# PSUM banks from a table, wider products for the old state, a longer overlap on GpSimd and another order in a chunked linear-attention and gated-MLP kernel

## Chip, core and metric

The kernel runs on one core of a Trainium2 chip. The metric is the device time of one execution in microseconds (us), taken as the median of several runs.

## What is computed

The first half is a linear attention whose state is a 40x40 matrix per head: 4 batches, 8 heads, 768 steps. The second half is an MLP with a spatial gate. Cut to what matters:

```python
for t in range(S):                                     # S = 768, D = 40
    y[:, :, t] = einsum('bhd,bhde->bhe', rt, state)
    Sa = einsum('bhde,bhe->bhd', state, at)
    state = state * wt[:, :, None, :] - einsum('bhd,bhe->bhde', Sa, bt)
    state = state + einsum('bhd,bhe->bhde', vt, kt)
x = y.transpose(0, 2, 1, 3).reshape(B, S, H * D)       # (4, 768, 320)
h = gelu_tanh(x @ w_in); u, v = halves(h)              # 320 -> 1024
v = layernorm(v) * g_ln
v = einsum('ts,bsd->btd', w_sg, v) + b_sg[None, :, None]
out = x + (u * v) @ w_out
```

## The kernel before

The 768 steps are cut into 12 chunks of 64 steps. Within a chunk the recurrence becomes products of matrices with a unit triangular 64x64 matrix per head, which has to be inverted. One unit of work is (c, b): chunk c, batch b, with 8 heads in 4 pairs (NP = 4). Everything in the attention is float32, so each product appears in the trace as two MATMUL records.

The stages of a chunk, with the names that the profile shows:

- The gates, `gate_w` to `gate_t`, work two to three chunks ahead. `gate_1` is a scan of decays on VectorE (`ex`), `gate_2` and `gate_3` scale the inputs (`at`, `kb`, with a second scan into `fixed`), `gate_4` is 32 MATMUL records into two PSUM tiles `ab0` and `ab1`, `gate_t` turns `kb` into the same two tiles. `gate_a` (VectorE), `gate_n` (ScalarE, into `nts`) and `gate_k` (ScalarE, into `kbt`) read those tiles and set them free.
- The inverse of chunk c covers all 4 batches at once. `inv_in` copies two blocks of `nts` on ScalarE, transposes them on VectorE into `n` (STREAM_TRANSPOSE) and sets the start of `x`. `steps` then walks 31 rows: every row is one multiplication into a scratch tile (`tg` for even chunks, `th` for odd ones) and one addition into `x`, both on GpSimd, each needing the one before. The last two rows are done on VectorE, then two transposes, `x1z` and `xt` (`inv_back`). `inv_g` (`gp`), a copy to `gs` on ScalarE (`inv_h`), `inv_x` (`xp`) and copies into `xt` (`inv_y`) finish it.
- `mixed(c, n)` sets GpSimd's order: the last 2*MIX operations of the chunk before (`behind`) are issued in turn with the first 2*MIX of this chunk, one of each, and the rest of this chunk follows alone.
- `chain1` to `chain5` carry the state: `ru` (two groups of products), `vu` on ScalarE, `sp`, `ut`, `pq`, `yp`, with `sc`, `pqs` and `yt` on VectorE and `vs`, `rhsb`, `s`, `vut` on ScalarE. `chain5` writes one PSUM tile `yp`: for every pair p and half h a product with `pqs`, and from chunk 1 on a product of the old state `s` with `rt`, 64 columns each.
- PSUM tiles come from `Banks`: one pool of 6 buffers in rotation during the attention (two more banks hold fixed tiles), 8 later. A tile waits until the tile that had its buffer has been read.

The order of instructions on each engine is fixed in the program. Every step gets a number by hand (tables `CH` and `LAG` for the chains, `GPOS` for the gates, `START` for `inv_in` and `mixed`, `BACK`, `GX` and `GL` for the end of the inverse, `DEC` and `DSTEP` for the splitting of `w_in`, `FILL` and `JUNK` for the first pieces of the MLP), 14 numbers to half a chunk and 28 to a chunk; `half(c, hf, side)` sorts the steps of half a chunk by these numbers and emits them. The numbers are no times: they only set the order. The start has the same in one list (`EX`, `T0` to `TX`, `W16`, `C1`, `SECOND`). `warmup` emits products of a zero tile into a PSUM tile `wp` that nobody reads; `HEADX`, `HEATX` and `HEAT` place them.

While the last inverse runs, `split64` starts to split `w_in` into two float32r parts (`DEC`), partly on GpSimd, through a staging tile `stg` with 3 buffers. All data moves by DMAs that SyncE issues, one queue in order. After chunk 12 `Mlp.run` works off the MLP pieces in the order of `SEQ0` and `SEQ`.

Of the kernel before, what the change touches and what calls it, by code (L numbers as in the profile page):

```python
# [9 lines left out]
F32 = mybir.dt.float32  # L10
# [22 lines left out]
HI_MAX = float(np.uint32(1151 << 20).view(np.float32))  # L33
FIRST = 0
FIRST1 = 0
EW = 1.12
WARM = (14, 0)
T0 = 7.05
T1 = 14.71
T2 = 3.18  # L40
TX = 17.97
LX = 4.92
YM = 64
HEAT = ((11.48, 11),)
# [10 lines left out]
T3 = 12.38
T4 = 17.94
CH = ((-17.8, 4.77, 22.83, 5.29, 40.56, 6.67, 11.98, 12.93, 5.11, 8.75, 12.38, 12.99), (-19.02, -6.94, 39.22, 1.7,
    27.65, 3.73, 7.69, 10.84, -17.0, 8.01, 8.38, 14.21))
GPOS = (((-18.02, -27.66, -4.05, -3.44, 7.45, 13.15, 8.8, 9.52, 9.57, 7.62), (-10.67, -0.89, -0.21, 1.03, 1.09, 8.16,
# [6 lines left out]
GE = ("VVVVV", "VVV", "V", "V")  # L66
START = (12.56, 6.02)
E0A = "GGGG"
E0K = "GVGG"
E1A = "GGGG"  # L70
E1K = "GGGV"
BACK = (20.27, 22.63, 24.69, 25.6)
GX = (25.56, 3.93)
CG = 0.7978845608028654
G1 = 0.044715
ENDS = {(9, 1): (("g", 0.01),), (10, 1): (("r", 0.01),), (11, 0): (("i", 5.0),)}
PIN = 266.02
DSTEP = ((-13.76, -2.78, -0.83, 0.94, 1.02, 4.34), (-10.29, 1.62, 1.75, 2.09, 4.54, 13.69))
DEC = ((264.82, 0), (278.5, 0), (286.65, 0), (289.18, 0), (281.75, 1), (296.38, 1), (293.09, 1), (312.42, 0), (313.95,
    0), (319.1, 1), (328.37, 0), (321.65, 1))  # L80
PX = 266.05
PV = 294.03
PL = 335.9
FILL = (('x0', 0, 321.07), ('v0', 0, 334.89), ('v1', 0, 335.46), ('v2', 0, 345.9), ('u0', 0, 355.78))
# [20 lines left out]
OSTEP = (-3, -1, 0, 0, 0, 0)  # L105
SGE = "GGGGGVGVVVVV"
OUTE = "VVGGGGGG"
SECOND = (32.86, 28.3)
ZERO = (-1, 39.49)
LAST = 2  # L110
MIX = 5
IS = 1
NS = 1
PQ = 1
MK = 40
JUNK = ((307.25, 5), (300.82, 4), (298.83, 6), (300.77, 3), (337.07, 1), (375.48, 3), (391.84, 4))
TP = 1
UT = 0
HEATX = (1000.0, 35.82, 1000.0, 39.48, 1000.0, 85.13, 48.06, 83.96, 1000.0, 1000.0, 1000.0, 166.1, 1000.0, 1000.0,
    1000.0, 1000.0)  # L120
HEADX = (17.16, 15.34, 14.51, 10.1, 1000.0, 24.98, 1000.0, 1000.0, 12.2, 1000.0, 4.58, 1000.0, 13.58, 1000.0, 17.09,
    6.6, 19.94, 1000.0, 19.57, 13.55, 8.17, -1.89, 1000.0, -1.97)
GL = (1.78, 1.2)
LAG = ((15.96, 0.95, -4.98, 0.45, 4.09, 1.29, (1.75, 9.96, -0.51, -0.16), (0.56, 10.54, 1.52, 2.45), 2.4, 1.22, 1.57,
    4.31), (6.29, 2.98, 6.71, 2.27, 9.49, 1.62, (0.64, 4.57, 1.17, 1.89), (5.92, 9.75, 3.57, 6.36), 14.35, 1.68, 5.0,
    8.49))
SEQL = ("s1", "s2", "s0", "s3", "s4", "s5", "s6", "s7", "o0", "o1", "o2", "o3", "o5", "o4")
ROWS = (12, 26)
EX = ((-0.41, 0, 0.35, 0.35, 1.61, 3.07, 2.57, 2.34, 1.25, 1.81), (0.76, 0, 0.75, 0.88, 1.87, 2.83, 3.55, 3.81, 2.13,
    1.97))  # L130


class Banks:

# [43 lines left out]
def attention(tc, a, xd, flag, keep, ps, mlp=None):  # L178
# [3 lines left out]
    V, A, G, T, Q = engines(tc)  # L182
    with ExitStack() as ctx:
# [32 lines left out]
        n = NP * (C + 1)  # L216
# [16 lines left out]
        x0 = iv.tile([128, NQ, 32], F32, name="x0")  # L233
# [72 lines left out]
        gate, unit, x1_of, st2, pqt = {}, {}, {}, {}, {}  # L306
# [1158 lines left out]
```

## Time and profile before

| what | us |
|---|---|
| median of 3 runs | 617.08 |
| runs | 617.08, 617.13, 614.1 |
| the profiled execution | 616.49 |
| span of its profile, first to last instruction | 614.7 |
| TensorE busy (PE) | 569.3 (93%) |
| VectorE busy (DVE) | 490.0 (80%) |
| GpSimd busy (POOL) | 367.3 (60%) |
| ScalarE busy (ACT) | 360.3 (59%) |

The mean granted TensorE clock is 0.956 of the full 2.4 GHz. Four stretches follow each other: a start up to about 73 us, chunks of 24 to 26 us each up to about 300 us, a change-over to the MLP until about 410 us, and the MLP, in which TensorE hardly pauses. The busy time of an engine hides two things that matter here: TensorE's records overlap in a pipeline, so the time from one record's start to the next is its cost and not its duration, and an engine can be short of time in one stretch while its share over the span is low.

### The profile page before, as it was taken

What the parts mean: (1) busy time and instruction counts of PE and PEld (TensorE: products, weight loads), DVE (VectorE), ACT (ScalarE), POOL (GpSimd) and SP (SyncE); (2) the same over time, 40 slices, a digit from 0 to 9 for tenths busy, and PEclk for the clock granted to TensorE, in tenths of its full rate; (3) what the DMA queues carried; (4) which work ended last, traced back from release to release, by engine and by line L of the source; (5) the groups of instructions that cost most, each with busy time, mean ns of one, the idle gap of its engine ahead of it and who ended that gap; (6) DMA issues with size and microseconds to landing.
All of it is one profiled execution on the core that took longest, in us unless ns stands there. A gap on an engine that the chain in (4) does not pass through costs nothing.

```text
span 614.7 us, 24521 instructions
## 1 busy us (share of the span) xinstructions
PE 569.3 (93%) x10136; PEld 519.4 (85%) x10136; DVE 490.0 (80%) x1083; ACT 360.3 (59%) x993; POOL 367.3 (60%) x844
## 2 busy tenths in 40 slices
PE   6888989999999999999976999699999999999995
PEld 5777878889888888887865879698999999999995
DVE  6958989989899899897855987898887679568632
ACT  5446777787787877877735736544453246224410
POOL 6738878888888888888883234455433432333230
PEclk9575999999999999999997999799999999999998
DMA  5613244544444445424415414510121103000002
GB/s 203 171 45 83 85 110 120 148 119 116 128 116 126 115 122 150 119 63 134 118 27 156 109 54 150 164 35 6 34 73 37 34 7 102 2 32 14 20 0 71
DMA packets 56889, 54.06 MB, mean 88 GB/s; under 512 B 35840, under 2 KB 47360, under 8 KB 56768
## 3 DMA queue, kind: packets, MB, share of 16 engines
q1 hardware_dynamic: 56768, 52.40, 30.8%
q8 instruction: 82, 1.34, 1.0%
q14 instruction: 39, 0.32, 0.2%
HBM read 44.52 MB, written 7.86 MB: 85 GB/s over the span
## 4 chain that ended last, share of the span: by engine, by line
PE 55%; DVE 25%; POOL 6%; issue 5%; ACT 4%; DMA 3%; SPq 1%; DVEq 0%; ACTq 0%; POOLq 0%
PE sg L164 13%; PE ru L164 6%; PE ab L164 5%; PE op L164 5%; PE hu L164 5%; PE hv L164 5%; DVE at L164 5%; PE pq L164 4%; PE yp L164 3%; DVE ex L164 3%; DVE fixed L164 3%; POOL x L164 2%; PE sp L164 2%; POOL th L164 2%; PE xp L164 2%
## 5 line engine op out<-in xcount | busy, mean ns | idle before, releaser
L164 POOL TENSOR_TENSOR th<-x,n 128x126 f32<-128x126 f32 (+21 forms) x174 | 66.4, 382 | 21.9 <-DVE n L164 11.7
L164 POOL TENSOR_TENSOR x<-x,th 128x126 f32<-128x126 f32 (+21 forms) x174 | 68.2, 392 | 9.7
L164 PE MATMUL sg<-wsh,vh 128*128 128x384 f32 x192 | 66.1, 344 | 5.6 <-ACT wsh L164 4.5
L164 POOL TENSOR_TENSOR gx<-g,gy 128x384 fp32r<-128x384 f32 x30 | 31.8, 1062 | 64.6 <-ACT gy L164 64.6
L164 PE MATMUL sg<-wsl,vh 128*128 128x384 f32 x192 | 65.8, 343 | 0.5 <-POOL wsl L164 0.5
L164 PE MATMUL sg<-wsh,vl 128*128 128x384 f32 x192 | 65.9, 343 | 0.0
L164 POOL TENSOR_TENSOR x<-x,tg 128x126 f32<-128x126 f32 (+25 forms) x160 | 60.0, 375 | 8.5
L164 POOL TENSOR_TENSOR tg<-x,n 128x126 f32<-128x126 f32 (+25 forms) x160 | 58.1, 363 | 11.3 <-DVE n L164 2.3
L164 PE MATMUL ab<-at,kb 64*64 64x64 f32 x1536 | 40.2, 237 | 13.9 <-DVE kb L164 6.5
L164 PE MATMUL pq<-rt,vut 128*64 128x128 f32 x768 | 52.4, 279 | 0.2 <-ACT vut L164 0.2
L164 DVE TENSOR_TENSOR at<-ab,mask 64x256 f32<-64x256 f32 x96 | 40.4, 421 | 11.8 <-PE ab L164 9.8
L164 PEld LDWEIGHTS ab<-at,kb 64*64 64x64 f32 x1536 | 33.3, 146 | 18.5 <-POOL kbt L164 4.3
L164 PE MATMUL yp<-pqs,kbt 128*64 128x64 f32 x768 | 46.8, 223 | 1.3 <-DVE pqs L164 1.3
L164 ACT CAST gy<-g 128x384 fp32r<-128x384 f32 x30 | 15.4, 514 | 55.4 <-DVE g L164 52.2
L164 ACT CAST vh<-v 128x512 fp32r<-128x512 f32 x24 | 14.9, 621 | 52.7 <-DVE v L164 52.7
L164 PE MATMUL yp<-rt,s 80*64 80x64 f32 (+1 forms) x704 | 43.5, 221 | 1.1 <-issue 1.1
L164 POOL TENSOR_TENSOR vl<-v,vh 128x512 fp32r<-128x512 f32 x24 | 31.4, 1312 | 21.2 <-ACT vh L164 21.2
L164 PEld LDWEIGHTS pq<-rt,vut 128*64 128x64 f32 x768 | 42.2, 139 | 2.1 <-ACT vut L164 0.4
L164 PEld LDWEIGHTS sg<-wsh,vh 128*128 128x128 f32 x192 | 36.9, 192 | 6.5 <-ACT wsh L164 4.8
L164 PEld LDWEIGHTS yp<-pqs,kbt 128*64 128x64 f32 x768 | 39.0, 138 | 2.1 <-DVE pqs L164 2.1
L164 DVE SCALAR_TENSOR_TENSOR g<-sg,gl,bt 128x384 f32<-128x384 f32 x32 | 19.7, 615 | 25.4 <-PE sg L164 24.3
L164 POOL TENSOR_TENSOR rs<-rs,mhalf 128x1 f32<-128x1 f32 x24 | 13.3, 554 | 42.4 <-DVE rs L164 37.1
(169 smaller groups left out, 1746.7 us busy)
## 6 DMA issues: line engine op xcount, KB each, us to landing
main<-main SPq DMA_DIRECT2D x88, 160.8 KB
vs<-vb SPq DMA_DIRECT2D x24, 160.0 KB
vu<-vs SPq DMA_DIRECT2D x24, 160.0 KB
rt<-rt SPq DMA_DIRECT2D x48, 80.0 KB
vut<-vt SPq DMA_DIRECT2D x24, 160.0 KB
xd<-yt SPq DMA_DIRECT2D x96, 40.0 KB
xt<-xd SPq DMA_DIRECT2D x16, 192.0 KB
out<-y SPq DMA_DIRECT2D x16, 192.0 KB
```

Source lines behind the costliest of these rows:

```text
L164: return self.tc.keep_in_program_order(f(*a, **k))
```

## The change

Four things change.

1. `Banks` makes one pool per PSUM bank. A string `BANK` of 503 digits says which bank the n-th tile takes; past its end it goes in rotation. `warmup(0)` takes no tile any more.
2. In `chain5` the old state's share is 4 products of 128 columns per (c, b) (both pairs of a half at once) in place of 8 of 64, and they come behind all products with `pqs`.
3. `MIX` is 7 in place of 5: the last 14 operations of an inverse on GpSimd are issued in turn with the first 14 of the next.
4. Nearly all numbers of the order are new. In the middle chunks, for chunk c in the steady state: TensorE takes `xp` ahead of `gate_4` of the first gate (it came behind `gate_t` of it), `ut` of the chunk's last batch directly behind `gp`, `gate_3` of the first gate on VectorE comes ahead of the next gate's `gate_1`, `n` on VectorE comes ahead of the scan and `kb` of the next gate, and on ScalarE `gate_n` of the last gate stands directly ahead of `inv_in`. At the start, of the 10 pairs of `wp` products that stood behind `chain1` and ahead of the inverse's first products, 6 stand ahead of `chain1` and 2 behind it.

```diff
-EW = 1.12
+EW = 1.14
-T1 = 14.71
+T1 = 22.43
-TX = 17.97
+TX = 22.86
-C1 = 9.42
+C1 = 15.98
-W16 = 3.35
+W16 = 7.12
-START = (12.56, 6.02)
+START = (11.84, 4.21)
-BACK = (20.27, 22.63, 24.69, 25.6)
-GX = (25.56, 3.93)
+BACK = (20.26, 24.86, 29.53, 27.62)
+GX = (26.85, 0.17)
-SECOND = (32.86, 28.3)
-ZERO = (-1, 39.49)
+SECOND = (55.53, 39.82)
+ZERO = (-1, 27.56)
-MIX = 5
+MIX = 7
-GL = (1.78, 1.2)
+GL = (1.02, 3.23)
...
-        self.rings = [ctx.enter_context(tc.tile_pool(name="ps", bufs=6, space=PSUM))] * 6
+        self.pools = [self.bank(i) for i in range(6)]
+
+    def bank(self, i):
+        return self.ctx.enter_context(self.tc.tile_pool(name=f"ps{i}", bufs=1, space=PSUM))
...
     def __call__(self, nm):
+        k = int(BANK[self.n]) if self.n < len(BANK) else self.n % len(self.pools)
         self.n += 1
-        return self.rings[self.n % len(self.rings)].tile([128, 512], F32, tag="ps", name=nm)
+        return self.pools[k].tile([128, 512], F32, tag="ps", name=nm)
...
                         T.matmul(yp[64 * h:64 * h + YM, o], lhsT=kbt[:, l0:l0 + YM], rhs=pqs[:, 4 * (p // 2) + 2 * h + p % 2],
-                                 start=True, stop=True, skip_group_check=True)
-                    for h in range(2 if c else 0):
-                        j = 2 * (p // 2) + h
-                        m = C if j < 3 else D
-                        T.matmul(yp[64 * h:64 * h + m, o], lhsT=st2[b][0:80].rearrange("p j x -> p (j x)")[:, D * j:D * j + m],
-                                 rhs=rt[0:80, p % 2, 2 * (p // 2) + h],
-                                 start=False, stop=True, skip_group_check=True)
+                                 start=not p, stop=True, skip_group_check=True)
+                for j in range(NP if c else 0):
+                    i, h = divmod(j, 2)
+                    m = C if j < 3 else D
+                    T.matmul(yp[64 * h:64 * h + m, 2 * C * i:2 * C * i + 2 * C],
+                             lhsT=st2[b][0:80].rearrange("p j x -> p (j x)")[:, D * j:D * j + m], rhs=rt[0:80, :, j],
+                             start=False, stop=True, skip_group_check=True)
```

`CH`, `LAG`, `GPOS`, `DEC`, `DSTEP`, `FILL`, `JUNK`, `HEADX`, `HEATX` and `EX` change in nearly every number.

## Rows read from the trace of the kernel before

**Rows 1.** Busy time by stretch; us per engine, records, granted clock, DMA.

```profile
147.80:172.45 24.65, 24.08 (x719) 21.39 (x716) 22.57 (x50) 19.68 (x63) 21.51 (x59) 1.00 0.48 124
...
430.00:602.00 172.00, 171.72 (x945) 165.45 (x946) 122.29 (x245) 66.92 (x135) 60.18 (x62) 1.00 0.11 33
```

**Rows 2.** GpSimd in order of time: start, duration, operation, shapes, idle before it.

```profile
142.21 0.24 POOL L164 TENSOR_TENSOR th<-x,n 128x31 f32<-128x31 f32 x1 [0.57 <-DVE n L164]
...
142.94 0.34 POOL L164 TENSOR_TENSOR tg<-x,n 128x78 f32<-128x78 f32 x1
143.24 0.23 POOL L164 TENSOR_TENSOR th<-x,n 128x30 f32<-128x30 f32 x1
...
147.38 0.32 POOL L164 TENSOR_TENSOR th<-x,n 128x78 f32<-128x78 f32 x1
147.78 0.33 POOL L164 TENSOR_TENSOR x<-x,th 128x78 f32<-128x78 f32 x1
...
171.36 0.27 POOL L164 TENSOR_TENSOR x<-x,th 128x45 f32<-128x45 f32 x1
...
172.01 0.32 POOL L164 TENSOR_TENSOR tg<-x,n 128x78 f32<-128x78 f32 x1
```

**Rows 3.** VectorE in order of time, from one x1z to the next.

```profile
147.83 1.09 DVE L164 STREAM_TRANSPOSE x1z<-x 128x512 f32<-128x512 f32 x1
...
163.00 0.69 DVE L164 TENSOR_TENSOR_SCAN fixed<-main,fixed 128x260 f32<-128x260 f32 x1
...
164.68 2.03 DVE L164 STREAM_TRANSPOSE n<-nts 128x1024 f32<-128x1024 f32 x1 [0.27 <-ACT nts L164]
...
172.45 1.10 DVE L164 STREAM_TRANSPOSE x1z<-x 128x512 f32<-128x512 f32 x1
```

**Rows 4.** TensorE in order of time, around one yp.

```profile
148.07 1.07 PE L164 MATMUL pq<-rt,vut 128*64 128x128 f32 x16
148.97 0.28 PE L164 MATMUL yp<-pqs,kbt 128*64 128x64 f32 x4
149.08 0.29 PE L164 MATMUL yp<-rt,s 80*64 80x64 f32 x4
```

**Rows 5.** Groups of the whole span: operation, count, busy us, mean ns, idle before.

```profile
L164 PE MATMUL pq<-rt,vut 128*64 128x128 f32 x768 | 52.4, 279 | 0.2 <-ACT vut L164 0.2
...
L164 PE MATMUL yp<-rt,s 80*64 80x64 f32 (+1 forms) x704 | 43.5, 221 | 1.1 <-issue 1.1
```

**Rows 6.** TensorE, then VectorE, then GpSimd, in the start.

```profile
32.22 7.55 PE L164 MATMUL wp<-warm 128*128 128x128 f32 x40 [0.59 <-ACT kbt L164]
39.70 1.26 PE L164 MATMUL g<-x1z,nts 32*32 32x16 f32 x128
...
34.99 1.07 DVE L164 STREAM_TRANSPOSE x1z<-x 128x512 f32<-128x512 f32 x1
...
43.48 0.24 POOL L164 TENSOR_TENSOR th<-x,n 128x31 f32<-128x31 f32 x1 [9.37 <-DVE n L164]
```

**Rows 7.** GpSimd behind the last inverse, and TensorE's next product.

```profile
321.15 0.72 POOL L164 TENSOR_TENSOR lt<-lt,sc 128x256 f32<-128x256 f32 x1
...
328.47 0.80 PE L164 MATMUL sp<-sc,ident 128*64 128x80 f32 x8 [8.91 <-DVE yt L164]
```

**Rows 8.** TensorE from gp to xp, and ScalarE's copies between them.

```profile
151.07 1.20 PE L164 MATMUL gp<-x1z,nts 32*32 32x32 f32 x64
152.20 0.38 PE L164 MATMUL ru<-ident,sc 104*80 104x104 f32 x2
...
154.05 0.42 PE L164 MATMUL ut<-ident,vu 64*80 64x64 f32 x4
155.04 0.79 PE L164 MATMUL ab<-at,kb 64*64 64x64 f32 x32 [0.57 <-DVE kb L164]
...
156.27 1.20 PE L164 MATMUL xp<-xt,gs 64*32 64x32 f32 x64
...
152.77 1.17 ACT L164 COPY gs<-gp 32x512 f32<-32x512 f32 x2
```

More of the change, by code (lines that the diff above doesn't have):

```diff
@@ L35 @@
 FIRST1 = 0
-EW = 1.12
+EW = 1.14
 WARM = (14, 0)
 T0 = 7.05
-T1 = 14.71
-T2 = 3.18
-TX = 17.97
-LX = 4.92
+T1 = 22.43
+T2 = 3.21
+TX = 22.86
+LX = 4.21
 YM = 64
-HEAT = ((11.48, 11),)
-LV = 5.9
-C1 = 9.42
-WP = 49.4
-W16 = 3.35
+HEAT = ((11.82, 11),)
+LV = 5.13
+C1 = 15.98
+WP = 48.52
+W16 = 7.12
 K16 = 0
-TB0 = -17.46
-TB1 = 16.05
+TB0 = -17.86
+TB1 = 9.57
 CUT0 = (2,)
@@ L54 @@
 ROWS0 = (0, 26)
[L55 to L59, printed above, removed]
[6 rows of a table removed]
+T3 = 8.39
+T4 = 13.75
+CH = ((-14.62, 4.41, 37.47, 6.14, 42.8, 6.77, 12.59, 14.12, 5.17, 9.44, 12.53, 13.26), (-19.81, -6.78, 54.8, 1.73,
+    31.86, 5.06, 7.1, 9.91, -38.88, 7.41, 7.11, 14.02))
+GPOS = (((-22.12, -20.64, -5.86, -5.21, 5.58, 10.09, 7.37, 7.65, 10.04, 6.33), (-18.63, -5.33, -1.99, -1.24, 1.25,
[6 rows of a table added]
 GE = ("VVVVV", "VVV", "V", "V")
-START = (12.56, 6.02)
+START = (11.84, 4.21)
 E0A = "GGGG"
@@ L77 @@
 PIN = 266.02
-DSTEP = ((-13.76, -2.78, -0.83, 0.94, 1.02, 4.34), (-10.29, 1.62, 1.75, 2.09, 4.54, 13.69))
-DEC = ((264.82, 0), (278.5, 0), (286.65, 0), (289.18, 0), (281.75, 1), (296.38, 1), (293.09, 1), (312.42, 0), (313.95,
-    0), (319.1, 1), (328.37, 0), (321.65, 1))
+DSTEP = ((-15.76, -2.54, -1.13, -0.3, 1.65, 2.2), (-13.56, -0.46, 1.98, 3.41, 7.44, 12.01))
+DEC = ((268.49, 0), (278.24, 0), (290.42, 0), (291.86, 0), (282.12, 1), (294.83, 1), (305.79, 1), (316.12, 0),
+    (310.87, 0), (320.78, 1), (326.62, 0), (327.2, 1))
 PX = 266.05
@@ L83 @@
 PL = 335.9
-FILL = (('x0', 0, 321.07), ('v0', 0, 334.89), ('v1', 0, 335.46), ('v2', 0, 345.9), ('u0', 0, 355.78))
+FILL = (('x0', 0, 320.4), ('v0', 0, 333.32), ('v1', 0, 334.58), ('v2', 0, 346.23), ('u0', 0, 360.21))
 AFTER = {"v": (0.56, 0.57, 1.47, 1.57, 2.13, 2.48, 2.96, 4.17, 5.19), "u": (1.14, 1.97, 2.82, 3.17), "x": ()}
@@ L115 @@
 MK = 40
-JUNK = ((307.25, 5), (300.82, 4), (298.83, 6), (300.77, 3), (337.07, 1), (375.48, 3), (391.84, 4))
+JUNK = ((299.01, 5), (309.84, 4), (315.19, 6), (310.85, 3), (346.94, 1), (390.81, 3), (380.55, 4))
 TP = 1
 UT = 0
[L119 to L122, printed above, removed]
-GL = (1.78, 1.2)
-LAG = ((15.96, 0.95, -4.98, 0.45, 4.09, 1.29, (1.75, 9.96, -0.51, -0.16), (0.56, 10.54, 1.52, 2.45), 2.4, 1.22, 1.57,
-    4.31), (6.29, 2.98, 6.71, 2.27, 9.49, 1.62, (0.64, 4.57, 1.17, 1.89), (5.92, 9.75, 3.57, 6.36), 14.35, 1.68, 5.0,
-    8.49))
+HEATX = (1000.0, 1000.0, 1000.0, 262.27, 143.53, 1000.0, 116.03, 1000.0, 1000.0, 200.3, 1000.0, 1000.0, 1000.0,
+    1000.0, 1000.0, 1000.0)
+HEADX = (1000.0, 13.61, -7.08, 1000.0, 4.3, 5.34, 13.95, 11.71, 1000.0, 1000.0, 6.17, 4.08, 1000.0, 8.27, 26.21, 8.84,
+    3.72, 15.74, 23.09, 1000.0, 10.42, -4.32, 14.21, 1000.0)
+BANK = ("0123450123435501250453111055152145231023102310214320321405302453145321045301502402315034310243524305"
+        "1243154102103541323510234023145023452410413524303541032103425103235034134250321253412041230541202512"
+        "3423051204052340134021534015412312054103051230423014523040530120145304245012431240351243523013045234"
+        "1453014201432501425120302345124026743510267345021763401547603215476031450762314537602145367025143670"
+        "2514367402531674203516740235167042315674023157604231576042135760421357604231576042315764023157642031"
+        "576")
+GL = (1.02, 3.23)
+LAG = ((14.43, 0.24, 9.68, 2.27, -1.01, 6.22, (1.2, 9.32, -0.5, 0.16), (3.56, 8.76, 1.4, 2.49), 1.04, 1.31, 1.83,
+    5.26), (2.38, 2.43, 10.19, 1.11, 11.42, 2.13, (0.98, 4.74, -0.31, 0.87), (3.63, 12.22, 3.84, 4.88), 9.33, 4.49,
+    2.76, 2.29))
 SEQL = ("s1", "s2", "s0", "s3", "s4", "s5", "s6", "s7", "o0", "o1", "o2", "o3", "o5", "o4")
 ROWS = (12, 26)
-EX = ((-0.41, 0, 0.35, 0.35, 1.61, 3.07, 2.57, 2.34, 1.25, 1.81), (0.76, 0, 0.75, 0.88, 1.87, 2.83, 3.55, 3.81, 2.13,
-    1.97))
+EX = ((-0.0, 0, 0.72, 0.75, 0.89, 3.06, 3.04, 3.4, 0.97, 1.22), (0.69, 0, 0.75, 1.04, 2.01, 2.7, 7.66, 4.43, 1.68,
+    2.1))
 class Banks:
@@ L145, in grow @@
     def grow(self):
-        if len(self.rings) == 6:
-            self.rings += [self.ctx.enter_context(self.tc.tile_pool(name="ps_more", bufs=2, space=PSUM))] * 2
+        if len(self.pools) == 6:
+            self.pools += [self.bank(i) for i in (6, 7)]
     def __call__(self, nm):
+        k = int(BANK[self.n]) if self.n < len(BANK) else self.n % len(self.pools)
         self.n += 1
-        return self.rings[self.n % len(self.rings)].tile([128, 512], F32, tag="ps", name=nm)
+        return self.pools[k].tile([128, 512], F32, tag="ps", name=nm)
 class InOrder:
@@ L253, in warmup @@
         def warmup(n):
+            if not n:
+                return
             wp = ps("wp")
```

12 rows, old and new, of the table GPOS are left out of this document.

## Prediction

> **What bounds the kernel now.** I read the busy time by stretch first. In a middle chunk of 24.65 us TensorE is busy 24.08, VectorE 22.57 and GpSimd 21.51, at the full clock [rows 1]. TensorE looks like the bound, so the next view is each engine in order of time. There the reader is to see that GpSimd, with the lowest of the three, has no room either: its 78-wide multiplication of one chunk starts at 147.38, that of the next at 172.01, a period of 24.63 us filled with operations that wait only for the one before; the 3 us that are not counted as busy are the gaps between them [rows 2].
>
> The chunks hang together in a loop, and VectorE's order shows it. From the end of `x1z` (147.83 + 1.09 = 148.92) to the end of `n` (164.68 + 2.03 = 166.71) pass 17.8 us [rows 3]. With `n` GpSimd can start on a chunk, and takes from 142.21 to 171.36 + 0.27 = 171.63, so 29.4 us, for it, its head and tail shared with the neighbours [rows 2]. From there to the end of `x1z` (172.45 + 1.10 = 173.55) it is 1.9 us [rows 3]. That `x1z` is two chunks behind the first one, because `n` is taken up two chunks ahead: (17.8 + 29.4 + 1.9) / 2 = 24.55 us a chunk, against 24.62 from `x1z` to `x1z`. So three limits lie within a tenth of each other: TensorE's own work (24.65 less one wait of 0.57 for `kb`, so 24.08 [rows 8]), GpSimd's (24.63), and the loop (24.55). Only what lowers all three shortens a chunk, to the highest of the new three.
>
> Behind the chunks, TensorE does nothing useful until 328.47, although the last inverse left GpSimd at 321.15, with the first split operation behind it [rows 7]. What follows hangs on GpSimd's end, so the end of the last inverse passes its shift on, whatever TensorE gained before. From 430 to 602 TensorE is busy 171.72 of 172.00 us [rows 1], with the same work before and after: that part only moves.
>
> **The products of the old state.** 44 units (c, b) lose 4 products of 64 columns pairwise, 352 of 704 records. The cost of a record is the distance of starts. 16 records of 128 columns in `pq` take 148.97 - 148.07 = 0.90 us, 56 ns each; 4 records of 64 columns in `yp` take 149.08 - 148.97 = 0.11, some 29 ns each [rows 4]. So a unit goes from 16 x 29 = 0.46 us to 8 x 56 = 0.45 us: 0.01 to 0.02 us, at most 0.08 a chunk and 0.9 us in all. The bounds are 0 and 0.9; I take 0.05 a chunk. The column of busy time says something else (43.5 us for 704 records, 62 ns each, against 52.4 for 768 of twice the width, 68 ns [rows 5]), but it counts the tail of the pipeline with whatever record is alone in it. The Trainium skill, "TensorEngine Tiling (Array Packing)", section Instruction Overhead, says that each matmul has about 60 cycles of overhead; at 2.4 GHz 352 records less would save an estimated 8.8 us, and the 29 ns between starts, of which 64 columns at one a cycle are already 27, speak against it.
>
> **Seven steps in turn on GpSimd.** Alone, a 78-wide operation costs 147.78 - 147.38 = 0.40 us from start to start, in turn with another chunk's 143.24 - 142.94 = 0.30 [rows 2]: the gap to its predecessor is filled. Two more steps are 4 operations on either side, 8 a chunk at about 0.10 to 0.13: 0.8 to 1.0 us less, so GpSimd's period becomes some 23.7. It has a price: a chunk's inverse now ends behind 4 more operations of the next one, so its own 29.4 us become about 1.0 longer. In the loop that is a loss.
>
> **The new order in the middle chunks.** `n` is moved ahead of the scan and `kb` of the next gate, which lie between 163.00 and 164.41 now (the start of `n` less its wait) [rows 3]: 1.4 us earlier, if `nts` is ready by then. `nts` is what `n` waits for already (0.27), and on ScalarE the copies in front of it (`kbt`, `at`, `vut`) are moved behind, so I take 1.4 whole; its bounds are 0, and 2.9 if VectorE's waits in that stretch go too, some 1.5 us by the difference of 24.65 and its busy time less small gaps [rows 1]. The loop then is (49.1 - 1.4 + 1.0) / 2 = 24.35 us, with the bounds (49.1 + 1.0) / 2 = 25.05 and 23.6. `xp` ahead of `gate_4` gives `kb` 1.13 us (156.27 less 155.04 holds `gate_4` and `gate_t`; `gp` shows 1.13 for a group as long as `xp`) and `gate_3` stands earlier on VectorE: the wait of 0.57 [rows 8] is covered. What is late next on TensorE is `xp` itself, costed under the rivals. TensorE's period is then 24.08 - 0.05 = 24.0. The highest of 24.0, 23.7 and 24.35 is the loop. I take 24.25, since a part of VectorE's waits goes with `kb`: 0.4 us less a chunk. From the first `x1z` of the loop to the last inverse there are 10 periods: 4.0 us, with 0 and 6.5 (24.0) as ends, and a loss where the loop stays at 25.05, for which `nts` would have to stay as late as now.
>
> **The banks.** The table frees TensorE from a fixed rotation. The trace names no long wait for a bank in the middle chunks: what remains of 24.65 us there beside the wait for `kb` is already busy time. I cost it at nothing, between -0.2 and +0.3 us a chunk. The plus is the second `ab` tile of the third gate, which takes the bank that `ut` of the same half held; between them stand only 16 records of `ru`, and ScalarE must have copied `vut` out.
>
> **The start.** TensorE issues 40 `wp` records from 32.22 to 39.70, 0.19 us each, and only then the inverse's first products `g`, while their input `x1z` ended at 34.99 + 1.07 = 36.06 [rows 6]. Of the 40, 24 now stand ahead of `chain1` and 8 behind: 8 fewer, 1.5 us, and the wait of 0.59 for `kbt` in front of them is covered by those moved. `g` would start at 39.70 - 2.1 = 37.6. At best it starts with `x1z`, 3.6 us earlier; at worst a later input takes over, 0. The first inverse in the loop starts on GpSimd at 43.48, behind 9.37 us of waiting for the second chunk's `n` [rows 6], and `n` stands behind a step on the result of `g`: it moves by the same 2.1. Its own inverse is 1.0 longer by the overlap, so 1.1 us remain (-1.0 to 2.6).
>
> **The change-over.** The split operations still stand behind the last inverse on GpSimd, and loads on SyncE's queue behind a load that waits for them; I cost the new order there at nothing, with 1.5 us to either side.
>
> **Sum.** 616.49 (the profiled execution) - 4.0 - 1.1 = 611.4; it stands 0.6 below the median of 617.08 and within the runs shown, so I keep 611.5 for the median.
>
> **Rivals.**
> - The loop opens further: VectorE's waits vanish and TensorE bounds, 24.0 a chunk, with a start that gains 2.6: 616.5 - 6.5 - 2.6 = 607.4. For it: `kb`, the cause of TensorE's wait, is also what VectorE's order brought forward. Against: `n` still needs ScalarE.
> - The products are worth what a fixed cost per record makes of them: by rows 5, 43.5 - 352 x 68 ns = 19.5 us, if TensorE alone were the bound, so 597 at the least; with the loop holding, this is cut to the 607 of the line above. The starts speak against it; the page above is its only other witness.
> - No change: `nts` is not ready earlier, and the loop takes up what the start gives. ScalarE's copies hang on `ab` of the last gate, and the products of that gate aren't moved ahead: 24.6 a chunk, 615 to 618.
> - Slower: TensorE waits for `xp`'s input. Today the copies `gs` end at 152.77 + 1.17 = 153.94 and `xp` starts at 156.27, so 2.3 us of cover [rows 8]. In the new order only `ut` (0.42 at most), `ru` and `yp` (152.20 to 154.05, 1.85) stand between them: `xp` is due some 2.2 us behind the end of `gp`, the copies 1.75 behind it, cover 0.4 to 0.5. On ScalarE `gs` stands behind a copy of the second transpose, which on VectorE is now behind a `yt`. Every microsecond that this chain is later than the cover stands in TensorE's period in place of the 0.57, with `gates`, `ru` and `pq` queued behind `xp`, and VectorE and ScalarE behind those. From 1.0 us a chunk on it costs: 24.0 + 1.0 = 25.0 is 0.4 above now. At 1.3 us, 10 chunks lose 7 and the start gives 1.1: 622.
>
> **How the numbers follow.** Forecast 0.46, opens further 0.16, products 0.03, no change 0.20, slower 0.15. A measurement of this kernel tells about 0.5%, 3.1 us, from no change. Faster by more (under 614): most of the forecast (0.41), the second and third: 0.60. Within: the rest of the forecast and most of the fourth: 0.24. Slower (over 620): 0.16. The range leaves out the third and most of the fifth: 605 to 619.
>
> **What would show it.** Right: `x1z` to `x1z` of 24.0 to 24.4 us; `n` ending about 16 us behind `x1z`; TensorE's wait for `kb` gone; 78-wide operations on GpSimd 0.30 apart; 32 records of `yp` and the old state still about 0.95 us a unit; `g` near 37.6; the first split operation on GpSimd near 316. Wrong: an idle time in front of `xp` named `gs`, a chunk of 24.6 or more with `n` waiting for `nts`, or a change-over that gives the 5 us back.

## The result and the profile after

The changed kernel takes 609.63 us (median; 607.4 to 617.28), beside 617.08 for the kernel before in the same runs: the ratio is 0.989, with an interval of 0.986 to 0.992. A later run of the unchanged new kernel beside the old one, among the experiments, gave 0.991 (0.988 to 0.994). The forecast was 611.5. One of the eleven executions, 617.28, fell in a slower state of the chip and is left out of the ratio. The profiled execution is 612.37 us, its span 610.6 against 614.7: the two profiles lie 4.1 us apart, the medians 7.4, and a profile can place only the 4.1.

Where these 4.1 us come from, by the times at which the same steps start (`hv` is the first product of the MLP):

| from - to | before | after | difference |
|---|---|---|---|
| start to the second `x1z` | 72.90 | 72.93 | 0.0 |
| to the eleventh `x1z` (9 periods) | 224.58 | 221.28 | -3.3 |
| to the first split operation behind the last inverse | 23.67 | 22.37 | -1.3 |
| to the last `x1z` | 11.23 | 8.52 | -2.7 |
| to the first `hv` | 20.2 | 24.9 | +4.7 |
| to the end | 262.1 | 260.6 | -1.5 |

The chunks gain 3.3, the start nothing, and the change-over gains 4.0 and gives 4.7 back. The nine periods differ between executions by as much as they gain: a second profile of the new kernel has 223.86 us there, and four of its variants below have 219.5 to 221.7.

First a middle chunk of after, busy time by stretch, and the MLP (columns as in [rows 1]):

```profile
146.09:170.34 24.25, 24.14 (x692) 21.39 (x687) 22.70 (x50) 19.61 (x62) 20.93 (x59) 1.00 0.47 126
426.00:598.00 172.00, 170.72 (x939) 164.18 (x939) 122.74 (x245) 68.02 (x138) 61.11 (x62) 1.00 0.11 32
```

TensorE is busy 24.14 of 24.25 us, VectorE 22.70, at the full clock. By this view, as by [rows 1], TensorE is the bound. It is not the one that sets the time, as the runs below show. The view that answers is VectorE in order of time with the waits in brackets: start, duration, operation, idle time before it and what ended that. This is one chunk of after:

```profile
146.09 1.09 DVE L174 STREAM_TRANSPOSE x1z<-x 128x512 f32<-128x512 f32 x1
...
160.01 2.05 DVE L174 STREAM_TRANSPOSE n<-nts 128x1024 f32<-128x1024 f32 x1
...
169.51 0.80 DVE L174 SCALAR_TENSOR_TENSOR x<-x,n 128x15 f32<-128x15 f32 x3 [0.93 <-POOL x L174]
170.34 1.08 DVE L174 STREAM_TRANSPOSE x1z<-x 128x512 f32<-128x512 f32 x1
```

And this is what stood in brackets in the chunk of before from 147.83 to 172.45, beside the 0.27 in front of `n` [rows 3]:

```profile
156.20 0.87 DVE L164 TENSOR_TENSOR at<-ab,mask 64x256 f32<-64x256 f32 x2 [0.36 <-PE ab L164]
...
161.18 0.85 DVE L164 TENSOR_TENSOR at<-ab,mask 64x256 f32<-64x256 f32 x2 [0.52 <-PE ab L164]
162.39 0.69 DVE L164 TENSOR_TENSOR pqs<-pq,mask 128x512 f32<-128x512 f32 x1 [0.36 <-PE pq L164]
```

Before, VectorE waited four times a chunk for TensorE and ScalarE, 0.36 + 0.52 + 0.36 + 0.27 = 1.51 us, and never for GpSimd. After, it waits once, 0.93 us, for GpSimd. Everything else on VectorE stands back to back, with gaps too short for the view to name (0.55 us in all before, 0.63 after): 24.62 - 1.51 = 23.11 us before, 24.25 - 0.93 = 23.32 after. So 0.58 us of waits went and 0.21 us of the rest came.

GpSimd in the same chunk of after, columns as in [rows 2]:

```profile
162.21 0.24 POOL L174 TENSOR_TENSOR tg<-x,n 128x31 f32<-128x31 f32 x1 [0.89 <-DVE n L174]
...
165.16 0.34 POOL L174 TENSOR_TENSOR th<-x,n 128x78 f32<-128x78 f32 x1
165.46 0.46 POOL L174 TENSOR_TENSOR tg<-x,n 128x56 f32<-128x56 f32 x1
...
169.21 0.27 POOL L174 TENSOR_TENSOR x<-x,th 128x45 f32<-128x45 f32 x1
```

The 78-wide operation that stood alone in [rows 2] is in the shared part now and costs 0.30 us from start to start, as forecast. But the shared part begins when `n` arrives (162.21) and the older chunk's inverse ends with it (169.48): from the start of `n` to the next `x1z` it is 10.33 us, against 172.45 - 164.68 = 7.77 in [rows 3].

The old state's products, TensorE in order of time (compare [rows 4]):

```profile
110.60 0.69 PE L174 MATMUL yp<-pqs,kbt 128*64 128x64 f32 x16
111.12 0.61 PE L174 MATMUL yp<-rt,s 80*64 80x128 f32 x8
111.56 0.45 PE L174 MATMUL sp<-sc,ident 128*64 128x80 f32 x8
```

This unit takes 111.56 - 110.60 = 0.96 us. Before, the same 16 records with `pqs` and 16 narrow ones took 164.21 - 163.25 = 0.96:

```profile
163.25 0.31 PE L164 MATMUL yp<-pqs,kbt 128*64 128x64 f32 x4
...
164.21 0.44 PE L164 MATMUL sp<-sc,ident 128*64 128x80 f32 x8
```

Single units vary with what follows them; the run with the old products in the new order, below, compares like with like. The wait for `kb` in front of `ab` [rows 8] is gone, and nothing waits in front of `xp` for `gs`.

The start, TensorE, first of after, then of before:

```profile
38.03 1.37 PE L174 MATMUL g<-x1z,nts 32*32 32x16 f32 x128 [0.31 <-DVE x1z L174]
...
43.07 0.24 PE L174 MATMUL y<-gz,xt 32*32 32x16 f32 x3 [1.89 <-issue]
46.52 0.24 PE L174 MATMUL x<-xt,gz 32*32 32x16 f32 x3 [1.46 <-issue]
```

```profile
43.46 0.17 PE L164 MATMUL y<-gz,xt 32*32 32x16 f32 x1 [0.72 <-issue]
46.91 0.18 PE L164 MATMUL x<-xt,gz 32*32 32x16 f32 x1 [2.21 <-issue]
```

`g` starts 1.67 us before the 39.70 of [rows 6]. Its input has become the limit: `x1z` itself starts at 36.81, 1.82 us later than the 34.99 of [rows 6]. Then the stalls named "issue" among the small products behind it grow from 2.93 to 3.35 us, and `x` starts only 0.39 us earlier. "issue" is idle time in which the engine waited for nothing that the profile shows; what the expectations below call instruction supply is this, and no run shows its cause.

The change-over of after: SyncE's queue, GpSimd behind the last inverse, and TensorE (compare [rows 7]):

```profile
302.86 0.62 SPq L174 DMA_DIRECT2D vut<-vt  x1
318.84 0.36 SPq L174 DMA_DIRECT2D stg<-w  x1
319.25 0.77 SPq L174 DMA_DIRECT2D xd<-yt  x2
320.11 0.53 SPq L174 DMA_DIRECT2D vs<-vb  x1
```

```profile
316.58 0.72 POOL L174 TENSOR_TENSOR lt<-lt,sc 128x256 f32<-128x256 f32 x1
```

```profile
323.01 0.86 PE L174 MATMUL ut<-ident,vu 64*80 64x64 f32 x4 [8.25 <-ACT vu L174]
```

For 15 us SyncE issues nothing: a load into the staging tile waits until GpSimd has read that tile, which it does behind the last inverse, and the moves of `yt`, `vs` and `vu`, which the last chunk's chain needs, are queued behind that load. TensorE stands 8.25 us. (In the kernel before, SyncE's queue stands 14.3 us in the same way, from 309.0 to 323.4.)

### The profile page after: what moved, and what is told of

Same layout as the page of the kernel before. It is cut to its first block, busy times and chain, and to the rows that moved or that the text cites. A ratio compares the mean times of both kernels' runs of the same rounds, so it can differ in the third digit from the quotient of the medians.

```text
span 610.6 us, 23787 instructions
## 1 busy us (share of the span) xinstructions
PE 566.4 (93%) x9784; PEld 515.1 (84%) x9784; DVE 489.5 (80%) x1083; ACT 359.0 (59%) x993; POOL 363.5 (60%) x844
## 4 chain that ended last, share of the span: by engine, by line
PE 62%; DVE 16%; POOL 7%; ACT 5%; issue 4%; DMA 3%; SPq 0%; DVEq 0%; POOLq 0%; ACTq 0%
PE sg L174 12%; PE ru L174 8%; PE ab L174 7%; PE op L174 6%; PE hu L174 6%; PE pq L174 5%; PE yp L174 5%; PE hv L174 4%; PE sp L174 3%; POOL x L174 3%; DVE at L174 2%; POOL th L174 2%; PE ut L174 2%; DVE fixed L174 2%; DVE ex L174 2%
## 5 line engine op out<-in xcount | busy, mean ns | idle before, releaser
L174 DVE SCALAR_TENSOR_TENSOR g<-sg,gl,bt 128x384 f32<-128x384 f32 x32 | 19.7, 615 | 25.3 <-PE sg L174 24.2
L174 PEld LDWEIGHTS sg<-wsl,vh 128*128 128x128 f32 x192 | 36.9, 192 | 1.0 <-POOL wsl L174 0.8
L174 DVE TENSOR_TENSOR pqs<-pq,mask 128x512 f32<-128x512 f32 x48 | 32.4, 677 | 6.1 <-PE pq L174 5.9
L174 PEld LDWEIGHTS sg<-wsh,vl 128*128 128x128 f32 x192 | 36.9, 192 | 0.0
```

Source lines behind the costliest of these rows:

```text
L174: return self.tc.keep_in_program_order(f(*a, **k))
```

## The experiments

**Is TensorE, or the products of the old state, the bound?** Both kernels without the old state's products.

```diff
-                    for h in range(2 if c else 0):
+                    for h in range(0):
```

> The kernel before, with the old state's products left out of yp (352 x 2 records less; the outputs lack that share). Theory of three limits: TensorE has 0.47 us a unit less to do, 1.9 a chunk, but GpSimd's order (24.63) and the loop from x1z over n to x1z (24.55) stay: x1z to x1z stays at 24.6 us, the ratio to before is 0.99 to 1.00 (a few us may come from the stretches outside the middle chunks). Rival, TensorE alone bounds the chunks: 22.8 to 23.0 us a chunk, ratio about 0.97. Rival, VectorE bounds: about 24.2 us, ratio 0.99.

Measured: 619.73 us beside 617.84, ratio 1.0035 (1.0009 to 1.006). The granted clock of these executions is lower, 0.934 to 0.952 against 0.949 to 0.956; in the chunk below it is full.

```profile
146.51:171.15 24.64, 22.84 (x656) 19.84 (x654) 22.59 (x51) 19.67 (x62) 21.51 (x59) 1.00 0.48 123
```

TensorE loses 1.2 us of work a chunk and the chunk stays at 24.64: neither TensorE alone (22.8 to 23.0) nor VectorE alone (24.2) sets it, as the two rivals have it. On VectorE the same four waits stand, 0.36, 0.52, 0.36 and 0.26: so they do not come from TensorE's load. That they are the length of the way from VectorE's inputs over TensorE and back fits TensorE's own wait for VectorE's `kb` in front of `ab` [rows 8].

```diff
-                for j in range(NP if c else 0):
+                for j in range(0):
```

> The changed kernel, with the old state's products left out of yp (the outputs lack that share). Theory: in the changed kernel TensorE bounds the chunks (24.1 to 24.4 us where no instruction supply stalls it), with GpSimd at 23.7 and the loop at 23.65 right behind it. So 1.8 us less work a chunk gives only 0.4 to 0.7: x1z to x1z of 23.6 to 23.8 us, some 4 to 6 us less than the changed kernel, ratio to before 0.978 to 0.983. Rival, the loop still bounds: no gain, ratio 0.988. Rival, TensorE is the only limit anywhere near: 22.4 us a chunk, ratio below 0.965.

Measured: 609.38 us, ratio 0.984 (0.980 to 0.989), too wide to tell the theory from "the loop still bounds". The chunks tell:

```profile
125.51:149.60 24.09, 22.73 (x655) 19.82 (x653) 22.57 (x51) 19.52 (x62) 20.92 (x59) 1.00 0.45 120
```

```profile
148.76 0.80 DVE L174 SCALAR_TENSOR_TENSOR x<-x,n 128x15 f32<-128x15 f32 x3 [0.92 <-POOL x L174]
```

The undisturbed chunks take 24.09 to 24.25, not the 23.6 to 23.8 that I expected. With TensorE busy 22.7 us only, VectorE still waits 0.92 for GpSimd, and 24.09 - 0.92 = 23.17 is VectorE's own again. TensorE's work sets the time of neither kernel.

**The width of the products.** The new kernel with the old 8 products of 64 columns.

```diff
-                for j in range(NP if c else 0):
-                    i, h = divmod(j, 2)
...
+                    for h in range(2 if c else 0):
+                        j = 2 * (p // 2) + h
...
```

> The changed kernel with the old state's products as before, 8 of 64 columns a unit, and all else new. Theory: 16 records at 29 ns cost what 8 at 56 ns do, 0 to 0.9 us over the whole kernel: the same time as the changed kernel, ratio to before 0.987 to 0.990, a unit of yp 0.95 us in both. Rival, a fixed cost of 25 ns a record: 8.8 us slower than the changed kernel, ratio 1.00. Rival, the busy time: 19 us slower.

Measured: 613.33 us beside 617.84, ratio 0.9936 (0.9913 to 0.9959), against 0.989 and 0.991 for the new kernel: above the 0.987 to 0.990 expected, and 0.3 to 0.5% (2 to 3 us) at the medians, with intervals that overlap. The profiles do not settle so small a cost: from the second `x1z` to the tenth it is 196.58 us, against 195.87 and 198.22 in two profiles of the new kernel. On TensorE itself, from the first record of a unit to the product behind it, the median of the 33 units without a wait between 75 and 300 us is 0.96 us with the narrow products and 0.93 with the wide ones: 0.03 a unit, 0.12 a chunk and 1.3 us in all if TensorE alone set the time. I had put it at 0.01 to 0.02 a unit and at most 0.9 us. The rivals of 8.8 and 19 us are out. The 8.8 us that the Trainium skill, "TensorEngine Tiling (Array Packing)", section Instruction Overhead, would give by estimate with its 60 cycles for each matmul are not there; that a unit loses 0.03 us with 8 records less, where 60 cycles each would be 0.2, speaks against that rule as a cost that is added to the columns.

**The overlap alone.** The kernel before with seven steps shared.

```diff
-MIX = 5
+MIX = 7
```

> The kernel before with MIX = 7 alone. Theory of three limits: GpSimd's order becomes 23.7 us a chunk, but a chunk's own inverse gets 1.0 us longer and the loop is (49.1 + 1.0) / 2 = 25.05: 0.4 us a chunk slower, 3 to 5 us, ratio 1.005 to 1.008, and GpSimd waits about 1 us for n in each chunk. Rival, GpSimd alone bounds: 0.9 us a chunk faster, ratio 0.985. Rival, TensorE alone bounds: 1.00, chunk time unchanged.

Measured: 647.62 us, ratio 1.048 (1.044 to 1.052): a loss of 30 us where I had expected 3 to 5.

```profile
132.18:159.37 27.19, 24.91 (x719) 21.99 (x716) 22.59 (x50) 19.69 (x61) 20.85 (x59) 1.00 0.41 114
```

```profile
158.54 0.80 DVE L164 SCALAR_TENSOR_TENSOR x<-x,n 128x15 f32<-128x15 f32 x3 [2.29 <-POOL x L164]
```

From `n` to `x1z` it is 10.3 us in every middle chunk, as in after: with four more shared operations on each side, 8 x 0.30 = 2.4 us more of GpSimd's work lie behind the arrival of the younger chunk's `n` and ahead of the end of the older chunk's inverse. VectorE needs that end at once, so the 2.4 us count whole in every chunk. (The shortest chunk takes 16.63 + 10.30 = 26.92; the others up to 29.7.) This is where my expectation failed: I had counted the four operations of the other chunk alone, 1.0 us, and halved them over two chunks.

**The overlap together with an earlier `n`.** As before it, and `gate_3` of the next gate moved behind `n` on VectorE, its `gate_c` (the copy `at`) and the copy `vut` behind the copies for `n` on ScalarE.

```diff
-MIX = 5
+MIX = 7
...
-(3.89, 5.06, 5.76, 11.59, 14.43, 19.14, 16.46, 16.46, 11.19, 14.61)
+(3.89, 5.06, 5.76, 12.6, 14.43, 19.14, 16.46, 16.46, 12.95, 14.61)
...
-(1.75, 9.96, -0.51, -0.16)
+(1.75, 9.96, -0.51, 0.8)
```

> The kernel before with MIX = 7, and with n ahead of the next gate's second scan and kb on VectorE and its copies ahead of vut and at on ScalarE. Theory of the short loop: from n to the next x1z 10.3 us as with MIX = 7 alone, from x1z to n 0.8 us less than there, 26.1 to 27 us a chunk: 5 to 10 us faster than MIX = 7 alone (647.6), so 637 to 643, still far slower than before. Rival, MIX = 7 is slow in the old order for another reason (TensorE's waits for kb, the banks): no change against 647.6.

Measured: 637.23 us, ratio 1.034 (1.028 to 1.040). In the shortest chunk `n` starts 15.83 us behind `x1z` instead of 16.85, and 10.33 later comes the next `x1z`: 26.16. The wait for GpSimd falls from 2.29 to 0.96.

```profile
155.99 0.80 DVE L164 SCALAR_TENSOR_TENSOR x<-x,n 128x15 f32<-128x15 f32 x3 [0.96 <-POOL x L164]
```

**The earlier `n` alone.** The two other lines of that diff without `MIX`. (The text says "three steps"; five are meant, the old overlap.)

> The kernel before with n moved ahead in VectorE's order, and the overlap left at three steps. Theory A, the short loop (the last x1z to n on VectorE, then the shared operations of GpSimd, then the next x1z) falls from 16.85 + 7.77 to about 14.0 + 7.8 = 21.8 and binds no more, but GpSimd's own order of a chunk, 24.63 at three steps, takes its place: n to x1z grows by what n comes earlier, the period stays at 24.6, the time at 615 to 618. Theory B, the order alone gives the gain: a period of 24.0 to 24.3 and 609 to 613.

Measured: 622.1 us beside 617.38, ratio 1.009 (1.007 to 1.011). Neither theory: the chunks take 25.3 us, and it is not GpSimd that takes over; it waits 1.05 us a chunk for `n`.

```profile
189.97 2.05 DVE L164 STREAM_TRANSPOSE n<-nts 128x1024 f32<-128x1024 f32 x1 [0.77 <-ACT nts L164]
```

`n` to `x1z` grows to 9.5 us without a wait in it: the operations that `n` was moved past now stand there, on VectorE. `x1z` to `n` falls by 1.0 only, since `n` waits 0.77 for `nts` instead of 0.27. With the old overlap, moving VectorE's work from one side of `n` to the other shortens nothing.

With this the time of a chunk in all these kernels, one chunk of each, can be laid out as VectorE's own order and what it waits for by name:

| kernel | chunk, from its `x1z` | length | VectorE's named waits | rest |
|---|---|---|---|---|
| before | 147.83 | 24.62 | 1.51 (TensorE 1.24, ScalarE 0.27) | 23.11 |
| before, no old state | 146.51 | 24.64 | 1.50 (the same) | 23.14 |
| before, 7 steps | 132.18 | 27.19 | 4.06 (GpSimd 2.29) | 23.13 |
| before, 7 steps and earlier `n` | 130.37 | 26.45 | 3.24 (GpSimd 0.96) | 23.21 |
| before, earlier `n` | 174.15 | 25.34 | 1.76 (GpSimd 0) | 23.58 |
| after | 146.09 | 24.25 | 0.93 (GpSimd) | 23.32 |
| after, no old state | 125.51 | 24.09 | 0.92 (GpSimd) | 23.17 |
| after, 6 steps | 145.04 | 24.19 | 0.47 (TensorE) | 23.72 |

The length goes from 24.1 to 27.2; the rest stays within 23.1 to 23.7. (In two chunks of "7 steps and earlier `n`" it is 25.2 and 25.4: one operation, `at<-main,ex`, took 2.33 us there instead of 0.41 to 0.66. Why stays open.) VectorE has the same operations in all of them, so that the rest is the same is no surprise and proves no limit by itself; no run here took work from VectorE.

What the runs do show is a loop of one chunk. Its first leg is VectorE's order from `x1z` to `n`. Its second leg leads from `n` to the next `x1z` and takes the longer of two things, VectorE's own work there and GpSimd's shared part. Before, the loop is 16.85 + 7.77, the second leg VectorE's; with 7 steps 16.89 + 10.30, GpSimd's; with the earlier `n` alone 15.81 + 9.52, VectorE's. In these three the first leg holds waits for TensorE and ScalarE, so the sum alone proves nothing; the lengthening of one leg by a run does. After, it is 13.93 + 10.33: in the chunk above the first leg holds no wait of VectorE, and in the second GpSimd runs from `n` to the last `x` without one. A closed loop without a wait in it is a limit.

**The overlap within the new order.** The new kernel once more, and with `MIX = 6`.

> The changed kernel once more, as the measure for the others of this group: ratio to before 0.986 to 0.992. Theory of the short loop (x1z to n on VectorE, then the shared operations on GpSimd until the inverse before ends, then the next x1z): from the start of n to the start of the next x1z 10.3 us in every chunk, and chunks of 24.1 to 24.4 us except where instruction supply stalls TensorE.

> The changed kernel with MIX = 6. Theory of the short loop: n to x1z becomes 9.1 us instead of 10.3, so the short loop is 14 + 9.1 = 23.1 us and no longer a limit; GpSimd's order is 24.15 us and TensorE 24.0 to 24.1, so the chunks take 24.1 to 24.2 us: 0 to 2 us less than the changed kernel in all. Rival, GpSimd's order was the limit that seven steps lifted: MIX = 6 gives half of it back, 0.5 us a chunk, 4 to 5 us slower than the changed kernel.

Measured: 610.87 (ratio 0.991, 0.988 to 0.994) and 610.2 (0.990, 0.987 to 0.994). With six steps `n` to `x1z` falls from 10.33 to 9.48 and VectorE no longer waits for GpSimd, but for `yp`:

```profile
146.77 0.42 DVE L174 TENSOR_TENSOR yt<-yp,ex 128x256 f32<-128x256 f32 x1 [0.47 <-PE yp L174]
```

Here TensorE is busy 24.12 of 24.19 us, so what GpSimd gives free it takes up at once: in the new order TensorE stands right behind the loop. The seventh step is worth nothing that can be measured; five steps in the new order were not run.

**The banks.** The new kernel with the old rotation of `Banks`.

> The changed kernel with the old rotation of six banks (later eight) in place of the table. Theory of the forecast, the banks are worth nothing by themselves: the same as the changed kernel within 0.5%. Rival, the new order needs the table: with a rotation its tiles wait for others that are read late (ut directly behind gp, pq early), TensorE shows waits of 0.3 us and more a chunk named vut, nts or kbt in front of ab, ut or yp, and the time is 4 us or more above the changed kernel.

Measured: 610.56 us, ratio 0.990 (0.986 to 0.994), as the new kernel with its table. In its profile TensorE waits nowhere between 75 and 300 us for `vut`, `nts` or `kbt`, the sign of the rival. Within the interval, some 2.5 us to either side, the table costs and brings nothing.

**The change-over.** The old kernel with the new constants of the change-over (`DEC`, `DSTEP`, `FILL`, `JUNK`).

> The kernel before with the new kernel's constants of the change-over alone (the due times and engines of the splits, the steps of the new state, the fills and the idle products). If the 4.0 us that after gains between its last two x1z is the change-over's own, the last x1z comes at 328 to 330 instead of 332.4, and the time is 613 to 617 as far as that lasts to the first hv. If it comes from the chunks' new order (GpSimd, done earlier), the last x1z stays at 331 to 334, and the time is 616 to 621.

Measured: 623.3 us beside 617.38, ratio 1.009 (1.007 to 1.011). The last `x1z` comes at 329.40 instead of 332.38, as after's constants promise (from the first split operation to it 8.7 us, as the 8.5 of after, instead of 11.2). But from there to the first `hv` it is 25.1 us, as the 24.9 of after and not the 20.2 of before. So both the gain and the loss of the change-over come with these constants. The whole is 6 us slower here, which it is not in after: most of it lies behind the first `hv` (267.3 us to the end against 262.1), where TensorE waits 3.87 us for `vut` in front of `pq`. Why it does so here and not in after stays open.

Then the new kernel without three groups of idle products, two of which stand on its chain of waits:

```diff
-JUNK = ((299.01, 5), (309.84, 4), (315.19, 6), (310.85, 3),
+JUNK = ((299.01, 5), (309.84, 0), (315.19, 0), (310.85, 0),
```

> The kernel after, with the three groups of idle products that its planner was to put into TensorE's stall ahead of the change-over (due 309.84, 315.19 and 310.85) left out. In the trace of after two of these groups stand behind the stall, at 333.6 (1.8 us) and 338.1 (1.6 us), on the chain of waits that ended last. Theory A, the idle products lie on the path and delay it by what they take: the first hv of the new state some 2 to 3.4 us earlier than 350.0, the time 607 to 609 against after's 610.9. Theory B, they only fill a time in which TensorE would wait for the weights' halves of VectorE and ScalarE (346 to 352) anyway: no change, 610 to 612. Theory C, without them the granted clock of 325 to 350 (0.93 in after) falls, and products take longer: 612 to 616.

Measured: 612.82 us, ratio 0.9925 (0.990 to 0.995): no gain. From the last `x1z` to `hv` it is 26.3 us. Where the idle products stood TensorE now waits for `pqs`, 1.79 us in front of `yp`; that they were on the chain did not mean that they delayed it. And the sign of theory C is there. From the last `x1z` to `hv`, before, after and in this run (the value behind ScalarE's and GpSimd's columns is the granted clock):

```profile
332.38:352.57 20.19, 19.90 (x513) 17.30 (x510) 16.24 (x42) 16.33 (x47) 3.59 (x5) 1.00 0.46 126
325.10:350.03 24.93, 24.77 (x520) 21.20 (x516) 18.70 (x48) 17.96 (x52) 5.99 (x8) 0.93 0.47 123
323.01:349.30 26.29, 23.94 (x506) 20.50 (x503) 18.75 (x48) 18.01 (x52) 5.99 (x8) 0.86 0.44 115
```

In after TensorE stood idle from 314.8 to 323.0, and the clock is at its lower level, 1.2 GHz, from 318.1 to 328.4, so the first 3.3 us behind the last `x1z` run at it; before, it is back at 2.4 GHz at 331.7, ahead of the last `x1z`. Without the idle products it falls a second time, from 340.7 to 344.1, behind the wait for `pqs`. So a part of the 4.7 us that the change-over gives back is this clock; how much, no run separates.

Last, without these products and with three splits moved from GpSimd to VectorE:

```diff
-(282.12, 1), (294.83, 1), (305.79, 1)
+(284.12, 0), (296.83, 0), (307.79, 0)
```

> As the run before, and three splits of the weights that after gives to GpSimd (due 282.12, 294.83 and 305.79) given to VectorE, 2 us later each. In after GpSimd comes to them only behind the last chunk's inverse, at 316.6, the weights' transfer follows (3.0 us), and TensorE stands 8.25 us until 323.0. Theory A, that stall ends with the split: TensorE restarts 3 to 7 us before 323.0, the last x1z falls from 325.1 to 319 to 323, and the time to 602 to 608. Theory B, the restart needs the inverse itself as well, or VectorE's order, 2 us longer in these chunks, makes the loop longer: the last x1z at 324 to 328 and the time 608 to 613.

Measured: **601.64 us** (600.37 to 604.46) beside 617.38, ratio 0.9745 (0.972 to 0.977): the best version, 11 us under the run before it, and what theory A said. Below is SyncE's queue, then TensorE's longest wait between 297 and 328, then VectorE's last `x1z`:

```profile
303.96 0.62 SPq L174 DMA_DIRECT2D vut<-vt  x1
306.46 0.36 SPq L174 DMA_DIRECT2D stg<-w  x1
306.87 0.82 SPq L174 DMA_DIRECT2D xd<-yt  x2
307.79 0.53 SPq L174 DMA_DIRECT2D vs<-vb  x1
```

```profile
309.88 0.69 PE L174 MATMUL yp<-pqs,kbt 128*64 128x64 f32 x16 [1.42 <-DVE pqs L174]
```

```profile
319.42 1.10 DVE L174 STREAM_TRANSPOSE x1z<-x 128x512 f32<-128x512 f32 x1
```

And from there to `hv`:

```profile
319.42:340.65 21.23, 19.22 (x478) 16.37 (x474) 18.55 (x51) 16.79 (x49) 1.43 (x2) 1.00 0.46 123
```

The load no longer holds up the queue (2.5 us instead of 16 from `vut` to `stg`), TensorE's 8.25 us shrink to 1.42, the last `x1z` comes 24.1 us behind the one before it, where after takes 30.9, and from there to `hv` it is 21.2 us, at the full clock, since the long stall ahead of it is gone. Against the run before it, 6.9 us come from the last period and 5.1 from the stretch to `hv`. That the eleventh `x1z` comes 3.3 us later than there (295.32 against 291.98; 294.21 in after) takes back a part.

## Why the forecast came out

The time was right, and the size of the main term fits; the reason for that term did not hold, and that its size fits is luck.

**The middle chunks: size right, limit wrong.** I had taken 0.4 us a chunk; from the second `x1z` to the tenth it is (199.01 - 195.87) / 8 = 0.39, and 0.10 in the second profile of the new kernel, in which the first of the eight chunks takes 26.39. The step that failed is "three limits lie within a tenth of each other", with the halving that follows from it. TensorE's 24.08 was none, as the run without the old state's products shows. VectorE's own order was left out because its busy time was the middle one (22.57 in [rows 1]), yet it is half of the loop of one chunk that the experiments show. And the third limit, (17.8 + 29.4 + 1.9) / 2 = 24.55, was none: its parts hold the waits. A way that leads from one chunk's `x1z` to that of two chunks later is two periods long whatever sets the period, so the sum had to come out. For after it does again: `x1z` ends at 122.47, `n` at 137.80, GpSimd takes that chunk up to 169.48, and `x1z` ends at 171.42, 48.95 / 2 = 24.5.

GpSimd's 24.63 was nearer to a limit than the table of VectorE's waits shows. Its first shared operation starts at 166.85, 0.14 behind the end of `n` (166.71 in [rows 3]), as close as in after, where it waits for `n` (162.06 and 162.21); and VectorE's last `x` starts at 171.71, 0.08 behind the end of GpSimd's (171.63 in [rows 2]):

```profile
166.85 0.24 POOL L164 TENSOR_TENSOR tg<-x,n 128x31 f32<-128x31 f32 x1
...
171.71 0.71 DVE L164 SCALAR_TENSOR_TENSOR x<-x,n 128x15 f32<-128x15 f32 x3
```

So before, GpSimd had some 0.1 us of room in a chunk. That both orders had to become shorter was right.

What moved, by this: `n` came 2.9 us earlier, 1.4 by the scan and `kb` that were moved behind it and 1.5 by VectorE's waits in that stretch, which I had named as the far bound ("if VectorE's waits in that stretch go too"): they went. Which of the new places opened them no run separates. Against the 2.9 stand 2.55 us for the longer overlap: 10.33 instead of 7.77 from `n` to `x1z`. By the undisturbed chunks that leaves 0.35 to 0.53 (24.63 to between 24.10 and 24.28); over all it is less in some executions, because the new kernel has chunks of 24.7 and 25.4, in one of which VectorE waits 1.17 for `pq` behind stalls of TensorE named "issue". In the sum I had halved both, as parts of a loop of two chunks, and taken the smaller gain: 0.7 where 2.9 came, and a price of 0.5 where 2.55 came. The two errors cancelled.

**GpSimd.** 0.30 a step in turn and an order of its own below 24: right. GpSimd waits 0.89 for `n` in the rows of after above, so its own order is 24.26 - 0.89 = 23.37, where I had 23.7. What I left out is for whom it works: the shared operations are the last thing that VectorE's `x` waits for.

**The products and the banks.** Right in kind: 0.12 a chunk at most on TensorE where I took 0.05 and 0.08 at most, and nothing that can be measured for the table.

**TensorE.** Its wait for `kb` is gone as forecast. That its end would not be the bound, as I had it, the runs without the old state's products show.

**The start.** Forecast -1.1, measured 0.0. `g` comes at 38.03 against the 37.6 forecast, but the second chunk's inverse starts on GpSimd only 1.12 us earlier (43.48 to 42.36), not 2.1. The next chunk's `n` comes 1.74 us earlier (64.37 to 62.63), and the overlap's price, put at 1.0, is 1.8 (8.53 to 10.30 from that `n` to the second `x1z`). That ate all of it.

**The change-over.** Forecast 0, and from the first split operation behind the last inverse (321.15 before, 316.58 after; near 316 was forecast) to the end it is 293.6 before and 294.0 after. But it is a sum of -2.7, +4.7 and -1.5, and I had looked for no such terms: here too the number is luck. What I had seen, "loads on SyncE's queue behind a load that waits for them", was on the way to the largest gain of any run here, and I priced it at nothing since both kernels have it.

**The rivals.** "The loop opens further" was right that VectorE's waits vanish, and wrong that only TensorE is left then: GpSimd's end was, with TensorE right behind it (the run with six steps). "The products are worth a fixed cost" and "TensorE waits for `xp`'s input" fell: no wait for `gs` stands in after. "No change" fell: in the middle chunk of after `n` waits for no `nts`. But neither half of the gain stands alone: in the old order the overlap costs 30 us, and the earlier `n` 5.

## What to carry over

A loop whose legs contain waits always sums to the period; it proves no limit, and neither does an engine's order whose rest stays the same because its work does. Look for a loop in which no leg holds a wait, and test it by a run that changes one leg: here 1.2 us less work on the engine with 98% of busy time left the chunk as it was, and 2.5 us more between `n` and `x1z` made it 2.3 us longer at the least. A longer overlap of two chains on one engine fills gaps, but it also puts the younger chain's work ahead of the older chain's end, and that counts whole where somebody waits for that end; and a queue that stands behind one load for 15 us deserves a look before any order in front of it is tuned.

## What the runs showed of the hardware

TensorE's stalls named "issue", 0.7 to 2.2 us, come in stretches of very many small products, in both kernels at the same places of the start (`y` and `x`, 32x16), and their sum grew from 2.93 to 3.35 us where the work in front of them came earlier. Their cause no run shows.

TensorE's granted clock followed its own stalls in the change-over. During the 8.25 us of idling in after it fell to 1.2 GHz, and it stood there from 318.1 to 328.4; in the version in which the longest stall there was 1.42 us it stayed at 2.4 GHz from 302 to 380 us.

GpSimd's operations can take longer while VectorE does the moved splits. Last inverse, in the version with three splits on VectorE and, behind it, in after:

```profile
315.22 0.48 POOL L174 TENSOR_TENSOR th<-x,n 128x78 f32<-128x78 f32 x1
315.78 0.41 POOL L174 TENSOR_TENSOR x<-x,th 128x78 f32<-128x78 f32 x1
```

```profile
313.61 0.34 POOL L174 TENSOR_TENSOR th<-x,n 128x78 f32<-128x78 f32 x1
314.03 0.34 POOL L174 TENSOR_TENSOR x<-x,th 128x78 f32<-128x78 f32 x1
```

From start to start 0.56 us against 0.42. The Trainium skill, "GPSIMD Engine Reference", section Specifications, says that GpSimd's way to SBUF is shared with VectorE and contended by VectorE's operations with two SBUF inputs. The first pair of rows fits that, since VectorE runs such an operation of a split beside it (`stg<-stg,sc`, from 315.42). But in the kernel before, `kb`, which has two such inputs as well, runs from 163.73 beside a GpSimd operation of the usual 0.40 us (164.07, 110 wide). No run here took the contention alone away, so the cause stays open.
